# A spectral filter followed by a low-rank token mixer: closing the first group on chip, reading the first weight ahead, and a new schedule for the first two batches

## The chip, the cores and the metric

The kernel runs on one core of one Trainium2 chip. The metric is the device time of one execution in microseconds (us). The trace's span is about 2 us shorter than the time of the same execution. "Step" is the program's own unit: one 512-token first-layer matmul pair with its ReLU, about 1.25 us; eight steps are a token group, six groups (and a shared small one) are a batch.

## The reference, cut to what matters

```python
# batch 8, seq 3136, dim 256; n_freq 1569; rank 32; hidden 1024
X = np.fft.rfft(x, axis=1)
y = np.fft.irfft(X * (filt_r + 1j * filt_i)[None], n=3136, axis=1)
h = y.transpose(0, 2, 1) @ U @ V                 # low rank, along the sequence
u = y + h.transpose(0, 2, 1)
out = u + np.maximum(u @ w_ch1, 0) @ w_ch2
```

The transform of length 3136 is done as 64 x 49 with matrix multiplications in four stages. Stage 1 is the "first weight" product. Then comes a transposition by way of DRAM (`ct1`: store, load back as "turned blocks" `a`); stage 2, the filter product and stage 3; a second pass through DRAM (`ct2`: store from `esb`, load back as `e`); stage 4, the inverse, which gives `ut`, the input of the two-layer network.

## The kernel before

TensorE executes its matmuls in program order. Work of later batches is laid between the network's steps by a plan: `at(step, function)`. The plan fixes only where an instruction stands in each engine's own queue. Batch 0 is different: it is turned on chip, and its filter product is done in an undoubled form.

```python
def load_x(b, c, after=None):          # on GpSimd's queue; converts f32 to f16
    ...
    t = sb.tile([128, 4, XW], F16, tag="x", bufs=4, name="x")
    if after is not None:              # gate: a one-element copy that waits for `after`
        nc.gpsimd.tensor_copy(t[0:1, 0, 0:1], after[0:1, 0:1])
    ...dma_start(...)
...
# batch 0: 16 half blocks; four of the products go to ScalarE + GpSimd
if j in (7, 9, 12, 14):
    nc.scalar.copy(pc, pz); nc.gpsimd.tensor_mul(uv, pc, fin)     # L397
else:
    nc.vector.tensor_mul(uv, pz, fin)                             # L400
...
mid_first()
load_e2(0, 0); load_e2(0, 1)           # from DRAM, after the last store
low_rank(0)
for n, _ in enumerate(st1(1)): ...     # all 13 pieces of batch 1's first weight
keep_warm(6)                           # dummy matmuls, L234
stage4(groups[0], 0); stage4(groups[0], 1)
make_fa(0); make_fa(1)                 # doubled filter matrices fa, fc
...
at(1, make_fa, 2); at(3, make_fa, 3)
at(4, x_after, 2)                      # x of batch 2, gated by groups[0].h[3]
m = later(start[b - 1], (5, -9, -12)[min(b, 3) - 1])   # batch 1's blocks from step 5
z = plan_mid(b, m, (2, 5) if b > 1 else (1, 3, 5))     # those listed: products on GpSimd
```

A block with its products on VectorE takes three 1024-column products (buffers `ta`, `tb`) and one addition on GpSimd. A block on GpSimd is copied out by ScalarE and then needs four GpSimd operations. Both are the doubled form, with matrices `fa` and `fc` that hold the filter twice. The undoubled form of batch 0 takes two products and no addition, but four more 512-column matmuls a block.

Three more words of this text: a bank is one of the eight parts of PSUM, the memory that TensorE writes its results to; an eviction is the copy out of it; the closing is the time from batch 0's last spectral output to the first ReLU.

Of the kernel before, what the change touches and what calls it, by code (L numbers as in the profile page):

```python
# [14 lines left out]
SEQ = 3136  # L15
# [9 lines left out]
def _consts():  # L25
# [10 lines left out]
    wf = np.zeros((128, 25, 128))  # L36
    for h in range(2):
        wf[h::2, 0:24, 64 * h:64 * h + 64] = t1[:, 24 * h:24 * h + 24]
    wf[0:64, 24, 0:64] = t1[:, 48]
# [59 lines left out]
    return (wf.reshape(128, 25 * 128).astype(f16), w2.astype(f16), g3.astype(f16),  # L99
# [4 lines left out]
def kernel(  # L104
# [13 lines left out]
    names = ("wf", "w2", "g3", "s4", "su", "tw", "kr")  # L118
    wf_d, w2_d, g3_d, s4_d, su_d, tw_d, kr_d = (
# [22 lines left out]
    def bank(tag):  # L142
        of = {"m": (0, 1), "o": (2, 3), "w": (4,), "e": (7,), "f": (0, 1, 2, 3, 4, 7), "e0": (7, 4), "f0": (0, 1), "w1": (7, 5, 6)}[tag]
        turn[tag] = turn.get(tag, -1) + 1
        return psum[:, of[turn[tag] % len(of)], :]


    NH = 17
    hring = cst.tile([128, NH, 512], F16, name="hring")
# [3 lines left out]
    wf = cst.tile([128, 25, 128], F16, name="wf")  # L153
    for c in range(4):
        i = slice(8 * c, min(8 * c + 8, 25))
        nc.sync.dma_start(wf[:, i], wf_d.rearrange("p (i m) -> p i m", m=128)[:, i])
# [3 lines left out]
    def load_x(b, c, after=None):  # L160
        if c == 3:
            t = sb.tile([64, DM], F16, tag="xl", bufs=2, name="xl")
            nc.gpsimd.dma_start(t, dram(x.tensor, (b * SEQ + 48) * DM, [[NR * DM, 64], [1, DM]]))
        else:

            t = sb.tile([128, 4, XW], F16, tag="x", bufs=4, name="x")
            if after is not None:
                nc.gpsimd.tensor_copy(t[0:1, 0, 0:1], after[0:1, 0:1])
            for h in range(2):
                nc.gpsimd.dma_start(t[h:128:2, :, 0:2 * DM],  # L170
                                    dram(x.tensor, (b * SEQ + 24 * h + 8 * c) * DM,
                                         [[NR * DM, 64], [2 * DM, 4], [1, 2 * DM]]))
# [6 lines left out]
    def load_filters(a, z):  # L179
# [8 lines left out]
        if z == NK:  # L188
            for p0, src in ((0, filt_r), (64, filt_i)):
# [8 lines left out]
    zero = cst.tile([128, 64], F16, name="zero")  # L198
    nc.vector.memset(zero, 0.0)
    nc.vector.memset(fb[96:128], 0.0)  # L200
    nc.scalar.copy(fb[32:64].rearrange("p s (k f) -> p (s k) f", f=64),
                   free(zero, 32, 64, 0, [[0, NK * DM // 64], [1, 64]]))
    nc.vector.memset(fc[:, 24:29, :], 0.0)
    usb = hflat[0:64, 0:NR * RANK]
    nc.gpsimd.dma_start(usb, moe_U.rearrange("(q r) p -> q (r p)", q=NQ))
# [4 lines left out]

# [7 lines left out]
    nc.scalar.dma_start(g3, g3_d.rearrange("p (f m) -> p f m", f=6))  # L218

# [3 lines left out]
    w2sb = cst.tile([128, 8, DM], F16, name="w2sb")  # L223
    vnat = hflat[64:96, 4704:4704 + SEQ]
    nc.gpsimd.dma_start(vnat, moe_V)
    nc.gpsimd.dma_start(w1sb, moe_w_ch1.rearrange("(h dd) c -> dd h c", h=2))

    sv = cst.tile([96, SEQ], F16, name="sv")
    kr = cst.tile([128, 96], F16, name="kr")

    def keep_warm(n):
        z = bank("f")
        for _ in range(n):
            nc.tensor.matmul(z, wf[:, 0, :], wf[:, 0:4, :].rearrange("p i m -> p (i m)"),  # L234
                             start=True, stop=True)
# [4 lines left out]
    def u_hat():  # L240
        ud = hflat[0:64, 1568:4704].rearrange("q (p c r) -> q p c r", c=2, r=NR)
        for p, eng in ((0, nc.vector.tensor_copy), (16, nc.scalar.copy)):
            eng(ud[:, p:p + 16], bass.AP(tensor=usb.tensor, offset=usb.offset + p,
                                         ap=[list(usb.ap[0]), [1, 16], [0, 2], [RANK, NR]]))
        for p in range(0, RANK, 8):
            z = bank("f")
# [4 lines left out]
            t = [sb.tile([98, NK, 8], F32, tag=tag, bufs=3, name="ut") for tag in ("ta", "tb")]  # L251
# [8 lines left out]
    def st1(b):  # L260
        for c in range(3):
            asb = sb.tile([128, 8, DM], F16, tag="asb", bufs=3, name="asb")
            for j in range(4):
                pf = bank("w" if b > 1 else "w1")
# [5 lines left out]
                if b == 1 and j % 2:  # L270
                    nc.vector.tensor_copy(dst, pf)  # L271
                else:
                    nc.scalar.copy(dst, pf)  # L273
# [5 lines left out]
            if 1 < b < NB - 1 and c:  # L279
                load_x(b + 1, c - 1)  # L280
            yield
        pf = bank("w" if b > 1 else "w1")
        nc.tensor.matmul(pf[0:64, 0:DM], wf[0:64, 24, 0:64], xt[b, 3], start=True, stop=True)
# [3 lines left out]
        if 1 < b < NB - 1:  # L287
# [5 lines left out]
    cm = fc.rearrange("p s d -> p (s d)")  # L293

    def turned(c):
        for g in range(0, 8 if c < 3 else 1, 4):
            for hh in range(2):
                z = bank("f")
                n, o = 512, 3136 * hh + (8 * c + g) * 128
                if c < 3:  # L300
                    for i in range(4):
                        nc.tensor.matmul(z[:, 128 * i:128 * i + 128],
                                         xt[0, c][:, (g + i) // 2, DM * (i % 2) + 128 * hh:DM * (i % 2) + 128 * hh + 128],
                                         wf[:, 8 * c + g + i, :], start=(i == 0), stop=True,
                                         skip_group_check=True)
                else:
                    n = 64
                    nc.tensor.matmul(z[:, 0:n], xt[0, 3][:, 128 * hh:128 * hh + 128],
                                     wf[0:64, 24, 0:64], start=True, stop=True)
                if hh:  # L310
# [3 lines left out]


    esb = {}
# [6 lines left out]
    def out3(b, k, half, pe):  # L323
        if half == 0:
            esb[b, k] = sb.tile([98, 4, DM], F16, tag="esb", bufs=10, name="esb")
        nc.scalar.copy(esb[b, k][:, 2 * half:2 * half + 2, :].rearrange("p s d -> p (s d)"),  # L326
                       pe[0:98])
        if half:
            nc.sync.dma_start(dram(ct2[b], 4 * k * 98 * DM, [[DM, 98], [98 * DM, 4], [1, DM]]),
                              esb[b, k])  # L330

    def stage3(pe, parts, special):

        for n, (v, m, ms) in enumerate(parts):
            kw = dict(start=(n == 0), stop=(n == len(parts) - 1))
            if special:
                nc.tensor.matmul(pe[0:98, 0:DM], g3[:, m, :], v[:, 0:DM], skip_group_check=True, **kw)
        if special:
            for n, (v, m, ms) in enumerate(parts):
                nc.tensor.matmul(pe[0:98, DM:2 * DM], g3[:, ms, :], v[:, DM:2 * DM], start=False,  # L340
                                 stop=(n == len(parts) - 1), skip_group_check=True)
        else:
            for n, (v, m, ms) in enumerate(parts):
                nc.tensor.matmul(pe[0:98], g3[:, m, :], v, start=(n == 0), stop=(n == len(parts) - 1))  # L344
# [8 lines left out]

    def mid_first():
# [3 lines left out]
        def turn_a2(k):  # L358
            z = bank("f0").bitcast(F16)
            for i in range(4):  # L360
                for hh in range(2):
                    nc.tensor.transpose(z[:, DM * i + 128 * hh:DM * i + 128 * hh + 128],
                                        free(fc, 0, 128, 3136 * hh + 4 * k + i, [[32, 128]]), idn)
# [4 lines left out]
            if k in (1, 3):  # L368
                nc.vector.tensor_copy(a2[k], z[0:98])
            else:  # L370
                nc.scalar.copy(a2[k], z[0:98])

        todo = []

        def do3(j, uv):
            pe = bank("e0")
            stage3(pe, [(uv[:, 0], 2, 4), (uv[:, 1], 3, 5)], j == 15)
            out3(0, j // 2, j % 2, pe)

        for k in range(4):  # L380
            turn_a2(k)
        for c in range(4):
            load_x(1, c)
        nc.gpsimd.dma_start(w2sb, moe_w_ch2.rearrange("(cc t) e -> cc (t e)", t=8))
        for j in range(16):
# [6 lines left out]
            fin = free(fb, 0, 128, 2 * j * DM, [[0, 2], [1, 2 * DM]])  # L392
            if j in (7, 9, 12, 14):
                pc = sb.tile([128, 2, 2 * DM], F16, tag="pc", bufs=2, name="pc")
                nc.scalar.copy(pc, pz)
                uv = sb.tile([128, 2, 2 * DM], F16, tag="y", bufs=3, name="uv")
                nc.gpsimd.tensor_mul(uv, pc, fin)  # L397
            else:
                uv = sb.tile([128, 2, 2 * DM], F16, tag="ta", bufs=3, name="uv")
                nc.vector.tensor_mul(uv, pz, fin)  # L400
            if j < 4:
                turn_a2(j + 4)
            todo.append((j, uv))
            if len(todo) > 3:
                do3(*todo.pop(0))
        while todo:
            do3(*todo.pop(0))


    h1 = {}  # L410
# [10 lines left out]
    def low_rank_end(b):  # L421
# [4 lines left out]
        nc.scalar.copy(h1[b][64:96, :], pk[64:96, 0:DM])  # L426
# [5 lines left out]
    def load_e2(b, c):  # L432
# [5 lines left out]
        nc.sync.dma_start(t[0:64], dram(ct2[b], 8 * c * DM, [[NR * DM, 64], [1, n * DM]]))  # L438
# [19 lines left out]
    def stage4(gr, dh):  # L458
# [23 lines left out]
        nc.vector.tensor_copy(o, v)  # L482
# [17 lines left out]
    def mm2_part(gr, t):  # L500
        b = gr.b
        if gr.c == 6:
# [3 lines left out]
            nc.tensor.matmul(o, gr.h[t][:, 0:128], w2sb[:, t, :], start=(t == 0), stop=False,  # L506
# [13 lines left out]
        for tt in range(4 * half, 4 * half + 4):  # L520
            nc.tensor.matmul(o, gr.h[tt][:, i * 128:(i + 1) * 128], w2sb[:, tt, :],  # L521
# [17 lines left out]
    fa = fb  # L539

    def make_fa(i):
        s = slice(8 * i, 8 * i + 8)
        nc.scalar.copy(fc[0:64, s], fb[64:128, s])
        nc.vector.tensor_scalar_mul(fc[64:128, s], fb[64:128, s], -1.0)
        nc.vector.tensor_copy(fa[64:128, s], fb[0:64, s])
        if i == 3:
            nc.vector.tensor_copy(fa[64:65, 31, :], fc[0:1, 31, :])
            for p in (0, 64):
                nc.vector.memset(fc[p:p + 1, 31, :], 0.0)


    keep_warm(10)
    u_hat()
    for c in range(4):
        turned(c)
        keep_warm(2)
    nc.sync.dma_start(sv[0:64], s4_d)
    nc.sync.dma_start(kr, kr_d)
    mid_first()
    load_e2(0, 0)  # L560
    load_e2(0, 1)
    nc.gpsimd.tensor_copy(sv[64:96, :].rearrange("p (r q) -> p r q", q=NQ),
                          vnat.rearrange("p (q r) -> p r q", q=64))
    low_rank(0)
    for n, _ in enumerate(st1(1)):
        if n == 3:
            low_rank_end(0)
        if n == 6:
            put_h(0, 0)
    load_e2(0, 2)  # L570
    load_e2(0, 6)
    keep_warm(6)
    stage4(groups[0], 0)
# [194 lines left out]
```

## Time and profile before

| | before |
|---|---|
| time, median of 3 runs (a fourth came beside the changed kernel) | 557.55 us (556.51 to 558.9) |
| span of the trace | 555.2 us |
| first ReLU | 62.6 us |
| batch 0's groups / batch 1's / the rest | 73.2 / 65.3 / 354.1 us |

The lines are in the prediction. How to read them: a row of forty digits is busy tenths by slice of the span; in a table of stretches each row is one interval with every engine's busy time, the granted TensorE clock and the share of the DMA engines' time; in a timeline the brackets tell how long the engine was idle before the instruction and what ended that.

### The profile page before, as it was taken

To read this page: it belongs to the slowest core of one execution; us is meant where nothing else is said; L and a number is where in the kernel's file an instruction comes from. 1 tells how busy PE (TensorE), PEld (TensorE's weight loads), DVE (VectorE), ACT (ScalarE), POOL (GpSimd) and SP (SyncE) were. 2 spreads that over 40 slices of the span, in tenths; PEclk is the share of its full clock that TensorE was granted. 3 is DMA by queue.
4 is the path that set the end of the run, shared out by engine and by line. 5 is a ranking of instruction groups with operands and counts; after the bars stand their busy time and mean duration, and the time that the engine had idled before them with its cause. 6 is when DMAs were issued, how large, how long until landed. Compare 5 with 4: busy or idle time off the path is not lost.

```text
span 555.2 us, 11638 instructions
## 1 busy us (share of the span) xinstructions
PE 517.2 (93%) x4491; PEld 375.3 (68%) x4491; DVE 353.1 (64%) x409; ACT 390.8 (70%) x684; POOL 282.4 (51%) x194
## 2 busy tenths in 40 slices
PE   5976689997999999999999999999999999999996
PEld 2634356664767777777776777777786777777775
DVE  6764675755756686758846785858746887643332
ACT  8566868774777688767776788677777577765663
POOL 5778179951883165915683175806563297300000
PEclk9999899997999999999999999999999999999999
DMA  9998876894669468774879468865653553333212
GB/s 194 157 170 192 225 141 187 209 230 130 174 184 250 125 176 199 173 204 137 193 222 221 123 173 228 166 199 152 186 170 121 141 167 121 106 113 115 96 77 87
DMA packets 85432, 92.06 MB, mean 166 GB/s; under 512 B 6741, under 2 KB 69416, under 8 KB 85376
## 3 DMA queue, kind: packets, MB, share of 16 engines
q1 hardware_dynamic: 67968, 75.12, 45.5%
q0 software_dynamic: 16960, 15.91, 19.1%
q8 instruction: 35, 0.57, 0.4%
q10 hardware_dynamic: 448, 0.28, 0.3%
q14 instruction: 21, 0.17, 0.1%
HBM read 57.42 MB, written 49.77 MB: 193 GB/s over the span
## 4 chain that ended last, share of the span: by engine, by line
PE 70%; POOL 10%; DVE 7%; DMA 6%; ACT 4%; issue 2%; DVEq 0%; ACTq 0%; POOLq 0%; SPq 0%
PE psum L521 25%; PE psum L488 24%; PE psum L352 4%; PE psum L344 4%; PE psum L477 4%; PE psum L497 3%; PE psum L266 3%; POOL y L634 3%; DMA x<-in_x_dram 3%; POOL x L170 2%; DVE ut L482 1%; DVE tb L632 1%; PE psum L416 1%; DMA w1sb<-in_moe_w_ch_dram 1%; ACT asb L273 1%
## 5 line engine op out<-in xcount | busy, mean ns | idle before, releaser
L492 ACT ACTIVATE hring<-psum 128x512 f16<-128x512 f32 (+1 forms) x416 | 237.7, 576 | 104.5 <-PE psum L488 103.2
L488 PE MATMUL psum<-ut,w1sb 128*128 128x512 f16 (+1 forms) x832 | 240.3, 370 | 6.4 <-ACT hring L492 3.0
L521 PE MATMUL psum<-w2sb,hring 128*128 128x256 f16 x1536 | 230.9, 273 | 0.0
L634 POOL TENSOR_TENSOR y<-ta,tb 128x1024 f16<-128x1024 f16 x56 | 120.5, 2159 | 159.4 <-DVE tb L632 115.5
L521 PEld LDWEIGHTS <-hring 128*128 128x128 f16 x1536 | 143.3, 98 | 63.8 <-issue 3.8
L482 DVE CAST ut<-psum 128x512 f16<-128x512 f32 x96 | 71.1, 741 | 108.3 <-PE psum L477 88.2
L488 PEld LDWEIGHTS <-w1sb 128*128 128x128 f16 x832 | 104.6, 145 | 27.3 <-issue 10.4
L529 DVE COPY och<-psum 128x512 f32<-128x512 f32 x96 | 66.2, 689 | 47.3 <-PE psum L497 46.6
L326 ACT CAST esb<-psum 98x512 f16<-98x512 f32 x128 | 74.7, 586 | 21.6 <-PE psum L344 16.0
L628 DVE TENSOR_TENSOR ta<-psum,fb 128x1024 f16<-128x1024 f32 x41 | 50.0, 1218 | 7.9 <-PE psum L352 6.9
L273 ACT CAST asb<-psum 128x512 f16<-128x512 f32 x78 | 45.7, 589 | 12.3 <-PE psum L266 11.2
L497 PE MATMUL psum<-idn,ut 128*128 128x128 f16 x392 | 54.0, 220 | 0.0
L477 PEld LDWEIGHTS <-e 96*128 96x128 f16 x768 | 35.9, 99 | 25.5 <-issue 10.2
L630 DVE TENSOR_TENSOR tb<-psum,fc 64x1024 f16<-64x1024 f32 x41 | 50.3, 1226 | 0.9
L632 DVE TENSOR_TENSOR tb<-psum,fc 64x1024 f16<-64x1024 f32 x41 | 49.9, 1218 | 0.8
L477 PE MATMUL psum<-sv,e 96*128 96x64 f16 x768 | 38.8, 194 | 6.5 <-DMA e<-ct 3.7
L344 PE MATMUL psum<-y,g 128*98 128x512 f16 x105 | 39.9, 380 | 3.0 <-POOL y L634 1.5
L497 PEld LDWEIGHTS <-ut 128*128 128x128 f16 x392 | 38.4, 98 | 4.9
L628 POOL TENSOR_TENSOR ta<-pc,fb 128x1024 f16<-128x1024 f16 x15 | 32.4, 2159 | 10.7 <-ACT pc L638 10.7
L352 PE MATMUL psum<-a,w2t 98*128 98x512 f16 x113 | 34.3, 379 | 1.7 <-DVE tb L632 1.6
L266 PE MATMUL psum<-x,wf 128*128 128x256 f16 x168 | 31.3, 274 | 2.8 <-DVE asb L271 1.0
L630 POOL TENSOR_TENSOR tb<-pc,fc 64x1024 f16<-64x1024 f16 x15 | 31.8, 2122 | 1.2
(93 smaller groups left out, 373.6 us busy)
## 6 DMA issues: line engine op xcount, KB each, us to landing
out_dram<-och SPq DMA_DIRECT2D x47, 512.0 KB
ct<-esb SPq DMA_DIRECT2D x64, 196.0 KB
x<-in_x_dram POOLq DMA_DIRECT2D x48, 256.0 KB, 8.1
e<-ct SPq DMA_DIRECT2D x48, 256.0 KB
a<-ct SPq DMA_DIRECT2D x56, 196.0 KB
ct<-asb SPq DMA_DIRECT2D x42, 256.0 KB
wf<-wf SPq DMA_DIRECT2D x3, 256.0 KB
w1sb<-in_moe_w_ch_dram POOLq DMA_DIRECT2D x1, 512.0 KB, 6.8
```

The source lines that it names most:

```text
L326: nc.scalar.copy(esb[b, k][:, 2 * half:2 * half + 2, :].rearrange("p s d -> p (s d)"), pe[0:98])
L344: nc.tensor.matmul(pe[0:98], g3[:, m, :], v, start=(n == 0), stop=(n == len(parts) - 1))
L477: nc.tensor.matmul(pu[:, 64 * i:64 * i + 64], e2[b, c][:, i, 128 * dh:128 * dh + 128], sv[:, 64 * r:64 * r + 64], start=(i == 0), stop=Tru ...
L482: nc.vector.tensor_copy(o, v)
L488: nc.tensor.matmul(ph[:, 0:n], w1sb[:, dh, :, t], gr.ut[:, dh, 0:n], start=(dh == 0), stop=(dh == 1))
L492: nc.scalar.activation(h[:, 0:n], ph[:, 0:n], RELU)
L497: nc.tensor.matmul(o[:, dh * 128:dh * 128 + 128], gr.ut[:, dh, t0:t0 + n], idn, start=False, stop=(dh == 1), skip_group_check=True)
L521: nc.tensor.matmul(o, gr.h[tt][:, i * 128:(i + 1) * 128], w2sb[:, tt, :], start=(tt == 0), stop=False, skip_group_check=True)
L529: nc.vector.tensor_copy(gr.och[:, 2 * y:2 * y + 2, :].rearrange("p j d -> p (j d)"), gr.pc)
L628: eng.tensor_mul(ta, p, va)
L630: eng.tensor_mul(tb[0:64], p[64:128], vb[64:128])
L634: nc.gpsimd.tensor_add(ys[k], ta, tb)
```

## The change

The intent: open the first group sooner. (1) The first weight comes compact (410 KB) and is doubled on chip. (2) All 16 products of batch 0 on VectorE. (3) 48 of the 64 blocks of group 0's input come early from DRAM, the last 16 are picked out of SBUF by selection matmuls. (4) Half of batch 1's x and the second layer's weight are loaded behind the low-rank result H; ten pieces of batch 1's first weight move into steps 0 to 10. (5) Batch 1 uses doubled matrices in four blocks only and takes the undoubled form in the other four, at steps 14 to 38. (6) x of batches 2 and 3 is planned at steps 12 to 16 and 40 to 45.

```diff
+    usb = ...; nc.sync.dma_start(usb, ...U...); nc.sync.dma_start(wfc, wf_d)       # compact
+    nc.vector.tensor_scalar_mul(wf[:, :, 64*h:64*h+64], wfc..., <0/1 per partition>)  # doubled
...
+            if j > 13: pick(j - 2)                     # selection matmuls, 4 column strips
+            if k == 5: load_e2(0, 0, 48)               # rows 0 to 47 early
...
+        for dh in range(2): for i in range(8):         # needs the early rows
+            nc.tensor.matmul(pu[dh]..., e2[0, 0][0:48, i, ...], sv[0:48, ...], ...)
+        step1(1); pick(14); low_rank_part(7); pick(15); ...; low_rank_end(0)
+            nc.tensor.matmul(pu[dh], zs[...], s4x, ...)
...
+    load_x(1, 2, h1[0])
+    nc.gpsimd.dma_start(w2sb[:, :, 0:DM], ...)
+    load_x(1, 3)
...
-        lead = (4, 8, 9)[min(b, 3) - 1]
+        if b == 1:
+            for k, q in ((0, 11), (3, 11), (2, 11), (5, 11), (1, 15), (4, 18), (6, 20), (7, 23)):
+                at(q, fetch, k)
+            for k, q, d in ((3, 17, 26), (2, 18, 28), (5, 22, 35), (4, 26, 37)): ...   # doubled form
+            for k, qs in ((0, (14, 15)), (1, (23, 24)), (6, (31, 32)), (7, (35, 36))):
+                ... two_q, mul_q (buffer tag "ta"), three_q                             # undoubled
...
-    at(4, x_after, 2)
+    for n in (0, 0, 1, 1, 2, 5, 6, 7, 8, 10): at(n, step1, 1)
+    for c in range(4):
+        at((12, 13, 15, 16)[c], load_x, 2, c); at((40, 42, 44, 45)[c], load_x, 3, c)
-            plan_st1(b, 12, (0, 1, 3, 4, 5, 7))
+            plan_st1(b, 20, (0, 1, 3, 4, 5, 7))
```

## The prediction

> **What bounds the kernel now.** I read the page first, then the busy time by stretches, then the chain that ended last, then the timeline of the opening. On the page (parts 1 and 2; one digit is 13.9 us):
>
> ```profile
> PE 517.2 (93%) x4491; PEld 375.3 (68%) x4491; DVE 353.1 (64%) x409; ACT 390.8 (70%) x684; POOL 282.4 (51%) x194
> ...
> PE   5976689997999999999999999999999999999996
> ...
> DMA  9998876894669468774879468865653553333212
> ```
>
> TensorE is full from the twelfth slice on. What it isn't, it is in the first six slices (83 us) and in slice ten (125 to 139 us), and there the DMA engines are near full. So there are two places to gain. To see how much, I cut the program at its token groups: eight ReLU steps (the ACT group of L492) make one group; the first group starts at 62.61 us in the timeline, batch 1's first at 135.81, batch 2's at 201.06, and so on. The stretches between those starts, one per batch:
>
> ```profile
> 62.60:135.80 73.20, 60.98 (x499) 42.34 (x498) 49.97 (x61) 51.09 (x88) 47.28 (x33) 0.95 0.76 179
> 135.80:201.05 65.25, 63.77 (x569) 46.98 (x567) 42.89 (x49) 49.37 (x93) 36.11 (x22) 1.00 0.70 182
> 201.05:260.55 59.50, 59.10 (x524) 43.59 (x523) 41.67 (x46) 44.48 (x81) 34.39 (x21) 1.00 0.71 185
> 260.55:323.69 63.14, 62.11 (x558) 46.12 (x557) 43.02 (x49) 47.27 (x91) 34.36 (x21) 1.00 0.72 186
> 323.69:383.20 59.51, 59.08 (x524) 43.56 (x523) 42.24 (x47) 44.48 (x81) 34.41 (x21) 1.00 0.71 183
> ```
>
> Columns: stretch, length, busy of PE, PEld, DVE, ACT, POOL with counts, granted clock, DMA share. Even batches have 48 steps, odd ones up to 56 (8 of them small). A quiet even batch takes 59.5 us with TensorE 99% busy; batch 0 takes 73.2 us although it has fewer TensorE instructions (499 against 524). From 201 us on nothing but TensorE counts.
>
> The time before 62.6 us: the chain that ended last shows what closes batch 0's spectral part and opens the first group:
>
> ```profile
> 47.42 0.61 PE psum L344 x2
> ...
> 48.69 1.08 PE psum L416 x32
> ...
> 57.03 2.72 PE psum L234 x6
> 59.75 0.44 PE psum L477 x8
> 60.21 0.74 DVE ut L482
> ```
>
> Between the last spectral matmul (47.4) and the first use of its result (59.75, L477) lie 12.3 us: the result goes to DRAM and comes back transposed, meanwhile batch 1's first weight product (L266) and six dummy matmuls (L234) fill the time. The product loop before that is uneven:
>
> ```profile
> 29.07 4.70 DVE L400 TENSOR_TENSOR uv<-psum,fb 128x1024 f16<-128x1024 f32 x4 [0.49 <-PE psum L344]
> 34.44 1.23 DVE L400 TENSOR_TENSOR uv<-psum,fb 128x1024 f16<-128x1024 f32 x1 [0.68 <-PE psum L352]
> 36.35 1.22 DVE L400 TENSOR_TENSOR uv<-psum,fb 128x1024 f16<-128x1024 f32 x1 [0.68 <-PE psum L352]
> 39.89 1.22 DVE L400 TENSOR_TENSOR uv<-psum,fb 128x1024 f16<-128x1024 f32 x1 [2.31 <-PE psum L352]
> ```
>
> VectorE does a product in 1.22 us when fed, but from 34 us on it waits, since in-order TensorE waits for the four products on GpSimd, which was itself still issuing DMAs until 36.6. And at the end of batch 0 the chain has the same round trip once more, for batch 1:
>
> ```profile
> 119.15 0.59 ACT esb L326
> ...
> 119.76 6.48 DMA ct<-esb
> ...
> 126.38 3.58 DMA e<-ct
> ...
> 130.09 0.60 PE psum L477 x8
> ```
>
> **What the Trainium skill says.** "TensorE: Matmul & The Clock Gate", Part 1 (the HAM clock gate): after an idle window of about 3.4 us the array runs at half rate. The trace agrees: after these holes the granted clock is 0.50 in 40 to 42 and 58 to 60 us and 0.72 in 130 to 140, and the six dummies took 2.72 us, 0.45 each, where a warm 512-column matmul starts every 0.22. "VectorE: DVE Perf Modes", the perf-mode tier table: a two-input operation with an f32 PSUM operand gets no fast mode, an SBUF f16 copy gets four elements a cycle. It agrees: 1.22 us for 1024 columns against 0.69 for a doubling copy of 2048. "GPSIMD Engine Reference", 4.1: two-input work is about twice as slow there; here 2.12 against 1.22 us. "DMA: Bandwidth & Descriptors", on issuing engines not being separate queues: all DMAs interleave on the same 16 engines; here the store of 119.76, which took 3.3 us from issue to the load behind it at 49.15 to 52.45, took 6.5 when four x loads had been issued at 109 to 112.
>
> **The change part by part.**
>
> 1. Arrival of x of batch 0. The first weight comes as 410 KB and is doubled on chip, instead of 819 KB; the 0.4 MB inverse matrix is asked for only inside the loop; two small constants (some 0.18 MB) are added; U no longer precedes x in the software queue. About 0.45 MB less stands before x; the first 20 us moved about 200 GB/s, so x, last landed at 19.2, lands about 2.2 us earlier. The doubling is two four-mode copies of 1536 columns on VectorE (about 0.55 us each by the 0.69 above), ahead of x. Only two transposed blocks instead of four precede the loop (-1 us), but the last quarter of the low-rank matrix (VectorE, 1.5 us by the row of 2 x 0.54 + 0.42) moves just in front of it. First product: 25.1 to about 22.4, -2.7.
>
> 2. The loop. All 16 products on VectorE: 16 x 1.22 + one block copy 0.69 = 20.2, and 1.8 for the last output matmul and eviction: about 22, against 25.1 to 49.1 = 24.0. TensorE needs per product 0.44 + 0.44, plus 0.67 of transposes in six of them, so it keeps up. -2. Batch 0's output is then whole at about 44.4 (before 49.1). Low-rank matmuls run inside the loop.
>
> 3. The closing. Of the 64 blocks, 48 come from DRAM early: their last store is issued after product 11, about 39; with 3.3 us to land and about 3.5 to load they are in at about 45.5. The last 16 are picked by selection matmuls (64 of 256 columns in four column strips; by L416's 32 in 1.06 us, about 2 us, mostly inside waits), without a round trip. After that: 16 small matmuls 0.8, low-rank eviction 0.37, a matmul 0.3, eviction 0.36, two matmuls with their latency 0.6, ut 0.74, first matmul pair and its latency 0.6, with queueing about 4.5. First ReLU at about 50, before 62.6: from the end of the output 5.6 instead of 13.5 us. Sum of 1 to 3: **-12.6**.
>
> 4. Batch 0's groups. TensorE work: the quiet 59.5, less the second matmuls that group 0 lacks (8 steps x 4 x 0.11 + residuals, -4.0), plus ten pieces of batch 1's first weight moved in here (10 x 0.24 = +2.4), plus the four blocks that use the undoubled filter form, 4 extra 512-column matmuls each (16 x 0.22 = +3.5): 61.4. VectorE: two products instead of three in those blocks saves 4 x 1.22 = 4.9, and the doubling of those four filter blocks goes to GpSimd and past step 30. ScalarE has 48 x 0.6 + 16 x 0.59 + 19 x 0.59 + 2 = 51 us: fits. The last spectral output is at step 38 instead of 40, and x of batch 3 is asked for from step 40 instead of before, so the store should land in about 3.3 instead of 6.5 us; with load about 7 to 8 us in the 8 steps of 1.25 (10 us) that are there. I leave 2.6 us for rough joints, the start with the e loads and w2 above all. 64 instead of 73.2: **-9.2**.
>
> 5. Batch 1: without the half clock in its first 5 us it should come near the other odd batch's 63.1; I take 63.7 for 65.25: **-1.5**. From 201 us the 354.1 us stay: TensorE is full, and 113 instead of 128 partitions change no duration.
>
> Sum: 50 + 64 + 63.7 + 354.1 = 531.8, plus 2.4 between profile span (555.2) and median time (557.55): **534 us**, -4.2%.
>
> **Rivals.** (a) The e load of the first 48 blocks is late. TensorE is in order and the small matmuls that need it stand before the selection matmuls, so each us of delay is one on the path. For: DMA share is about 1.1 in 32 to 46 us, and stores queue behind waits on one queue. Against: half of batch 1's x and w2 are moved out of just this stretch. Worth +3 to +5: 538. (b) The second matmul's weight, issued only when the low-rank result exists, takes 13.6 us to land as it did behind x before, and group 1 waits for it: +2 to +5. Against: then about 1.8 MB of x were queued ahead, now 0.5 MB. (c) The gain of the opening is given back at batch 1's start: the round trip still doesn't fit, or GpSimd, with eight doubling copies and x issues between, is late: +4 to +7, and the clock falls again; about 540. (d) TensorE, now carrying 5.9 us of added matmuls in batch 0, is no worse than before because it was idle there 12 us: that is already in part 4; if the joints are perfect, 530. (e) A quite hidden gain, time unchanged: against it, from 201 us on the chain is TensorE alone, so an earlier start has nowhere to be lost.
>
> **Range and chances.** Parts 1 and 2 I trust to 2 us, 3 to 3, 4 to 4: together some 6. Range 527 to 543. Faster by over 2% needs under 546.4: 0.94; within 2% 0.05; slower 0.01.
>
> **What would show it.** First ReLU at 48 to 53 us; 16 products on VectorE back to back from about 22.4; no dummy matmuls after the loop; granted clock 1.0 after the first 10 us; batch 0's stretch 62 to 67 us; no e wait over 1 us near the start of batch 1; the time from batch 2's start to the end still 354 us. Wrong, if the first ReLU comes after 55, if a wait on DMA of several us stands before L477's successor or the first second matmul, or if the steady batches change.

## The result, and the profile after

The changed kernel took **571.9 us** (570.57 to 573.75, 4 runs); before, beside it, 558.12. Slower by 2.5%: ratio 1.0253, 95% interval 1.021 to 1.0296. Ratios here are the mean time of one kernel's fast runs over that of the other's of the same rounds, so not quite the ratio of the medians.

The page after, parts 1 and 2 (a slice is 14.2 us):

```profile
PE 522.2 (92%) x4535; PEld 374.6 (66%) x4535; DVE 355.9 (63%) x414; ACT 374.9 (66%) x677; POOL 279.2 (49%) x200
...
PE   5897748777899999999999999999999999999997
...
PEclk9896969989999999999999999999999999999999
...
DMA  9996944557769855895489467784755534333212
```

TensorE was busy for only 4 tenths of slice six and 7 to 8 tenths of slices seven to ten; before, these digits were 8, 9, 9, 9 and 7. By stretches, cut at the groups' first ReLUs as before (batch 0, batch 1, batch 2; then groups 1, 3 and 4 of batch 0):

```profile
53.58:149.51 95.93, 69.81 (x534) 46.33 (x533) 52.15 (x65) 48.87 (x87) 43.62 (x37) 0.92 0.70 161
149.51:214.58 65.07, 64.03 (x570) 47.05 (x569) 42.77 (x48) 50.12 (x95) 40.61 (x25) 1.00 0.71 183
214.58:274.14 59.56, 59.17 (x524) 43.54 (x523) 41.62 (x46) 44.53 (x81) 34.41 (x21) 1.00 0.71 184
```

```profile
61.03:83.23 22.20, 11.33 (x81) 7.40 (x81) 9.68 (x18) 5.14 (x9) 1.17 (x2) 0.77 0.79 171
...
95.75:113.08 17.33, 13.23 (x101) 8.74 (x99) 9.10 (x9) 10.52 (x21) 12.65 (x7) 1.00 0.56 153
113.08:132.55 19.47, 15.31 (x104) 9.72 (x102) 9.94 (x12) 11.06 (x21) 4.91 (x6) 0.91 0.50 115
```

The first ReLU does come 9 us sooner (53.59 for 62.61), but batch 0's groups take 95.9 us instead of 73.2; everything later is as long as before (65.1 and 354.5 us). Busy time overstates TensorE's use, since the records of matmuls overlap (L588's last 371 ns each, where a warm one starts every 0.22 us). So I also made an estimate: every matmul at N / 2.4 GHz + 2.5 ns, which the Trainium skill gives for warm matmuls ("TensorE: Matmul & The Clock Gate", Part 1), with 60 columns as the least. A steady batch of 59.5 us comes out at 60.2, so this is good to about 1 us. Batch 0's useful stream rose from 58.3 to 63.6 us; the loss, length less stream, rose from **14.9 to 32.3 us**. By group the loss after is 2.0, 12.9, 1.3, 5.1, 6.9, 4.0 us.

The clock in the closing, by stretches of 2 us (the third figure from the end of a row):

```profile
44.00:46.00 2.00, 0.00 (x0) 0.00 (x0) 0.24 (x1) 0.00 (x0) 0.00 (x0) 0.73 0.75 195
46.00:48.00 2.00, 1.57 (x22) 1.08 (x26) 0.00 (x0) 0.00 (x0) 0.00 (x0) 0.50 0.71 199
...
54.00:56.00 2.00, 2.00 (x10) 1.12 (x9) 1.78 (x3) 0.94 (x3) 2.00 (x3) 0.71 1.15 177
```

Cut finer, it is 1.00 until 44.9, 0.50 until 55.1 and 1.00 again from 55.2 us.

The largest hole, in the timeline of the changed kernel: TensorE, then the sync queue, then GpSimd's queue.

```profile
79.13 1.01 PE L385 MATMUL psum<-a,w2t 98*128 98x512 f16 x2 [10.26 <-DMA a<-ct]
```

```profile
54.80 12.28 SPq L299 DMA_DIRECT2D ct<-asb  x6
67.18 3.02 SPq L537 DMA_DIRECT2D e<-ct  x1
70.31 0.54 SPq L308 DMA_DIRECT2D ct<-al  x1
76.19 1.63 SPq L348 DMA_DIRECT2D a<-ct  x4
```

```profile
57.47 3.74 POOL L187 DMA_DIRECT2D x<-in_x_dram  x6
61.87 0.99 POOL L180 DMA_DIRECT2D xl<-in_x_dram  x1 [0.67 <-DMA w2sb<-in_moe_w_ch_dram]
```

Step 14 needs a turned block of batch 1 and waits 10.26 us for it. The last store of the first weight (32 KB) is issued at 70.31, and the loads behind it may go only at 76.19. Meanwhile the engines carry x of batch 2, the last of which lands at 74.18: GpSimd issues it at 57.5, during step 4, although the plan has it at steps 12 to 16. Nothing tied GpSimd to TensorE's steps there. In the DMA part of the profile between 55 and 79 us the software queue, which carries x and until 61.6 us the second weight, has 61.3% of the engines' time, the hardware queue 36.6%:

```profile
q0 software_dynamic: 2959, 2.28, 61.3%
q1 hardware_dynamic: 3571, 2.32, 36.6%
```

The other holes are of another kind. Timeline of the changed kernel in group 3:

```profile
94.19 4.20 POOL L720 TENSOR_TENSOR y<-ta,tb 113x1024 f16<-113x1024 f16 x2
...
96.34 1.23 DVE L743 TENSOR_TENSOR uv<-psum,fb 113x1024 f16<-113x1024 f32 x1 [1.32 <-ACT hring L592]
97.62 0.59 PE L385 MATMUL psum<-a,w2t 98*128 98x512 f16 x2 [1.53 <-DVE uv L743]
...
98.42 1.22 DVE L743 TENSOR_TENSOR uv<-psum,fb 113x1024 f16<-113x1024 f32 x1 [0.85 <-POOL y L720]
...
104.92 2.12 POOL L720 TENSOR_TENSOR y<-ta,tb 113x1024 f16<-113x1024 f16 x1
107.08 1.22 DVE L714 TENSOR_TENSOR ta<-psum,fb 113x1024 f16<-113x1024 f32 x1 [4.83 <-PE psum L597]
```

Each of these VectorE products starts when a GpSimd addition ends (94.19 + half of 4.20 = 96.29; 98.39; 107.04), whatever the bracket names. All three write a buffer of tag `ta`, and the addition is that buffer's last reader: a block on GpSimd holds a `ta` buffer for some 8 us, and an undoubled block takes two.

At the end of batch 0 TensorE waits for the first turned block of batch 2, while x of batch 3 had been issued from 117.39 on (GpSimd, then TensorE):

```profile
117.39 1.31 POOL L187 DMA_DIRECT2D x<-in_x_dram  x2
```

```profile
139.03 0.59 PE L385 MATMUL psum<-a,w2t 98*128 98x512 f16 x2 [3.04 <-DMA a<-ct]
```

### The profile page after: what moved, and what is told of

Its sections match the earlier page's. It is cut to its first block, busy times and chain, and to the rows that moved or that the text cites. A ratio compares the mean times of both kernels' runs of the same rounds, so it can differ in the third digit from the quotient of the medians.

```text
span 569.1 us, 11725 instructions
## 1 busy us (share of the span) xinstructions
PE 522.2 (92%) x4535; PEld 374.6 (66%) x4535; DVE 355.9 (63%) x414; ACT 374.9 (66%) x677; POOL 279.2 (49%) x200
## 4 chain that ended last, share of the span: by engine, by line
PE 70%; POOL 9%; DMA 7%; DVE 5%; issue 4%; ACT 3%; SPq 0%; ACTq 0%; POOLq 0%; DVEq 0%
PE psum L621 26%; PE psum L588 25%; PE psum L385 4%; PE psum L377 4%; PE psum L597 3%; PE psum L577 3%; PE psum L291 3%; DMA x<-in_x_dram 2%; POOL x L187 2%; POOL y L720 2%; DMA w2sb<-in_moe_w_ch_dram 2%; DMA a<-ct 1%; POOL sv L464 1%; PE psum L515 1%; DVE tb L718 1%
## 5 line engine op out<-in xcount | busy, mean ns | idle before, releaser
L588 PE MATMUL psum<-ut,w1sb 128*128 128x512 f16 (+1 forms) x832 | 241.4, 371 | 1.9 <-DVE ut L582 1.1
L720 POOL TENSOR_TENSOR y<-ta,tb 113x1024 f16<-113x1024 f16 x52 | 112.1, 2161 | 146.0 <-DVE tb L718 129.9
L582 DVE CAST ut<-psum 128x512 f16<-128x512 f32 x94 | 69.7, 741 | 98.6 <-PE psum L577 82.4
L588 PEld LDWEIGHTS <-w1sb 128*128 128x128 f16 x832 | 104.6, 145 | 24.4 <-issue 6.8
L295 ACT CAST asb<-psum 128x512 f16<-128x512 f32 x76 | 44.9, 590 | 22.1 <-PE psum L291 21.1
L385 PE MATMUL psum<-a,w2t 98*128 98x512 f16 x120 | 37.9, 394 | 21.6 <-DMA a<-ct 13.3
L714 DVE TENSOR_TENSOR ta<-psum,fb 113x1024 f16<-113x1024 f32 x37 | 45.1, 1219 | 16.6 <-PE psum L385 7.7
L714 POOL TENSOR_TENSOR ta<-pc,fb 113x1024 f16<-113x1024 f16 x15 | 32.3, 2155 | 34.2 <-ACT pc L724 34.2
L716 DVE TENSOR_TENSOR tb<-psum,fc 49x1024 f16<-49x1024 f32 x37 | 45.4, 1226 | 0.9
L718 DVE TENSOR_TENSOR tb<-psum,fc 49x1024 f16<-49x1024 f32 x37 | 45.1, 1218 | 1.0
L377 PE MATMUL psum<-y,g 113*98 113x512 f16 x98 | 37.4, 382 | 2.1 <-ACT esb L355 1.1
L577 PE MATMUL psum<-sv,e 96*128 96x64 f16 x752 | 37.3, 192 | 1.6 <-ACT asb L295 1.6
L291 PE MATMUL psum<-x,wf 128*128 128x256 f16 x168 | 33.1, 281 | 2.3 <-DVE ut L582 1.9
L716 POOL TENSOR_TENSOR tb<-pc,fc 49x1024 f16<-49x1024 f16 x15 | 31.8, 2120 | 1.2
```

Of the source, the lines that this page charges most:

```text
L385: nc.tensor.matmul(pz, w, a, start=True, stop=True)
L577: nc.tensor.matmul(pu[:, 64 * i:64 * i + 64], e2[b, c][:, i, 128 * dh:128 * dh + 128], sv[:, 64 * r:64 * r + 64], start=(i == 0), stop=Tru ...
L582: (nc.scalar.copy if gr is groups[0] and dh else nc.vector.tensor_copy)(o, v)
L588: nc.tensor.matmul(ph[:, 0:n], w1sb[:, dh, :, t], gr.ut[:, dh, 0:n], start=(dh == 0), stop=(dh == 1))
L714: eng.tensor_mul(ta, p[0:NZ], va)
L716: eng.tensor_mul(tb[0:NR], p[64:NZ], vb[64:NZ])
```

## The experiments

"Before" was run beside each of them (medians 555.95 to 557.08 us). Losses and stretches are from each run's own trace, one per edit. The changed kernel was not run beside them, so compare the ratios; the intervals of e1 (1.0106 to 1.0237) and e11 (1.0113 to 1.0281) overlap its own, and what these two show is in their traces.

| run | edit | median us | ratio to before | first ReLU | batch 0's groups |
|---|---|---|---|---|---|
| changed kernel | | 571.9 | 1.0253 | 53.6 | 95.9 |
| e1 | x of batch 2 gated | 566.8 | 1.0172 | 52.9 | 92.2 |
| e2 | own buffer for GpSimd blocks | 563.6 | 1.0114 | 52.3 | 89.7 |
| e3 | e1 + e2 | 561.2 | 1.0067 | 53.6 | 86.7 |
| e4 | e load behind the last store | 571.1 | 1.0249 | 53.0 | 96.9 |
| e5 | e3, six evictions to VectorE | 562.3 | 1.0118 | 53.7 | 86.3 |
| e6 | e3, batch 1's x early | 559.0 | 1.0059 | 58.0 | 79.4 |
| e7 | e5 + e6 | 557.4 | 1.0029 | 56.4 | 79.6 |
| e8 | new opening, schedule of before | 570.0 | 1.0251 | 60.0 | 87.1 |
| e9 | e2, and loads put around the round trips | 552.2 | 0.9926 | 54.0 | 76.4 |
| e10 | e9, other steps for the single bank | **550.1** | **0.9899** | 53.8 | 74.6 |
| e11 | changed kernel, no selection matmuls | 567.6 | 1.0197 | 53.2 | 90.2 |
| e12 | e10, no selection matmuls | 555.7 | 1.0001 | 52.8 | 76.8 |

**e1, e2, e3, e4: the two holes and a rival for the first.** Theory A: x of batch 2, issued ten steps early, fills the DMA engines while batch 1's first product makes its round trip. Rival B: the last store merely stands behind an e load in the sync queue. Theory C: shared product buffers. Rival D: VectorE is overfull.

```diff
# e1
-        at((12, 13, 15, 16)[c], load_x, 2, c)
+        at(15, x_after, 2, c)        # load_x(2, c, groups[1].h[7] if c == 0 else None)
-            plan_st1(b, 20, (0, 1, 3, 4, 5, 7))
+            plan_st1(b, 21, (0, 1, 3, 4, 5, 7))
# e2
-            box[k] = [pz] + [sb.tile(..., tag="ta", bufs=3, name="ta"), tbs[...]]
+            pool = k in ((3, 5) if b == 1 else on_pool)
+            ta = sb.tile(..., tag="tp" if pool else "ta", bufs=1 if pool else 3, name="ta")
# e4
-        at(8 * c - 14, load_e2, 0, c)
+        at(12 if c == 3 else 8 * c - 14, load_e2, 0, c)
```

> Edit: the x loads of batch 2 on GpSimd's queue get a gate (they wait for the ReLU of step 15, i.e. until the first use of batch 1's turned blocks), batch 2's first weight starts at step 21 instead of 20. Theory A (GpSimd, which nothing holds back, issues these 1.5 MB at 57.5 us, ten steps ahead of the plan, and they fill the DMA engines while batch 1's first product makes its round trip): TensorE's wait of 10.3 us for the turned block falls to 2 to 4 us, the clock stays at 1.0 there, time about 571.9 - 9 = 563 us (560 to 566). Rival B (the store of the last block stands behind the e load on the sync queue, whatever else runs): the wait stays at 8 us or more, time within 3 us of 572. Theory C (shared product buffers) touches only what comes after 90 us: the waits there stay.

> Edit: only the blocks whose products run on GpSimd get a buffer of their own for the first product; the VectorE products keep the three of before. Theory C (the slow GpSimd blocks hold the three buffers which the undoubled blocks on VectorE now take twice each): VectorE's waits of 1.3, 0.85 and 4.8 us at 96, 98 and 107 us go, TensorE's behind them (1.5 at 97 and part of 110 to 116) too: -3 to -6 us, about 567; the wait of 10.3 us at 69 us is as before. Rival D (those holes come from VectorE being overfull, with negations slowed by GpSimd): within 2 us of 572.

> Edits of e1 and e2 together. If A and C are both right and independent: about 572 - 9 - 4.5 = 558.5 (554 to 562), still not faster than before by 2%, since a wait of about 3 us for the turned block and the crowded end of batch 0 stay. If A alone holds: as e1.

> Edit: one e load (group 3 of batch 0) is planned at step 12 instead of 10, so that it no longer stands before the store of batch 1's last first-weight block on the sync queue; x of batch 2 ungated. Rival B: the store is issued about 3 to 5 us earlier and TensorE's wait of 10.3 falls by that, about 567 us. Theory A: the two large stores of 64.2 and 64.9 us are stuck in the full DMA engines anyway, the wait stays at 8 us or more, time 570 to 573.

In e1 (566.58 and 567.08 us) TensorE's line at step 14 reads

```profile
73.39 1.01 PE L385 MATMUL psum<-a,w2t 98*128 98x512 f16 x2 [5.58 <-DMA a<-ct]
```

so the wait fell from 10.26 to 5.58 us and the time by about 5, less than the 9 I expected. In e4 it stayed at 9.00 (571.15 and 571.14 us), though the store was issued 3.9 us sooner, at 66.43: the loads behind it still went only at 75.93. In e1, without x, they went 4.1 us after it (66.27 to 70.39). So what holds them is the traffic in front, not the place of the small store. Theory A is right in direction and rival B falls, but A is only half of the hole: with x out of the way, one round trip still doesn't fit into the four steps from 10 to 14. In e2 (563.27 and 563.96 us) groups 3 and 4 fell from 36.8 to 30.9 us, the wait at step 14 stayed (10.20). That is theory C, somewhat stronger than expected. The edit adds a fourth buffer, so it shows that buffers were short; whether three unshared ones would do is not tested. 1.3 us of e2's gain is an earlier first ReLU, which the edit doesn't explain: in its trace the clock fell at 47.9 us instead of 44.9, so that more of the closing ran at full clock. Both together (e3) gave 561.2, not the 558.5 of the sum. (A version of e2 with three more buffers did not fit into SBUF.)

**e5, e6, e7: what is left in e3?** Theory E: ScalarE is crowded. Theory G: half of x behind H leaves the round trip too few steps.

```diff
# e5, on e3: batch 2's first weight, six of twelve evictions to VectorE
+ {1: (0, 3, 4, 5, 7, 8, 9, 11), 2: (3, 4, 6, 9, 10, 11)}
# e6, on e3
-        for c in range(2): load_x(1, c)
+        for c in range(4): load_x(1, c)
-    load_x(1, 2, h1[0]) ... load_x(1, 3)
-    for n in (0, 0, 1, 1, 2, 5, 6, 7, 8, 10): at(n, step1, 1)
+    for n in (0, 0, 1, 1, 2, 2, 3, 3, 4, 5): at(n, step1, 1)
```

> Edit on top of e3 (561.2 us): six of the twelve evictions of batch 2's first weight go from ScalarE to VectorE. Theory E (the packed schedule gives ScalarE three evictions in many of the steps 20 to 38, 1.8 us of work against 1.25 us of TensorE's, and in-order TensorE waits for their banks): groups 3 to 5, 14.6 + 16.6 + 17.8 = 49.0 us in e3, fall by 3 to 5, time about 557. Rival F (the pair of product banks and VectorE set the pace there, not ScalarE): groups 3 to 5 within 1.5 us of 49 or longer, time 560 to 563.

> Edit on top of e3: the second half of batch 1's x is loaded ahead of the low-rank result again, and the ten remaining pieces of batch 1's first weight stand at steps 0 to 5 instead of 0 to 10. Theory G (half of x behind H leaves the round trip of batch 1's first product only four steps): TensorE's wait of 5.2 us for the turned block goes (under 1 us), group 1 falls from 16.3 to about 11; the e load of the closing meets the x load and the first ReLU comes 1 to 3 us later than 53.6. Time about 557 (555 to 559). Rival: the gain is all given back in the closing (first ReLU at 58 or later), time 560 to 563.

> Edits of e5 and e6 together on top of e3: about 561 - 4 - 4 = 553 us if both theories are right, 557 if one, 561 if none.

e5: groups 3 to 5 took 14.80 + 17.40 + 17.55 = 49.75 us against 49.04 in e3, the time 561.53 and 563.07. Theory E falls. e6: the wait at step 14 is gone and group 1 took 9.3 instead of 16.3 us, so G is right about that; but the closing paid:

```profile
50.85 1.03 PE L486 MATMUL psum<-sv,e 48*128 48x64 f16 x16 [9.03 <-DMA e<-ct]
```

This is the wait for the early rows of group 0, 2.99 us in the changed kernel, 9.03 here. The sync queue of e6 shows why: a store issued at 37.77 lets the load behind it go only at 47.74, while batch 1's x and the second weight are in flight.

```profile
37.77 1.22 SPq L362 DMA_DIRECT2D ct<-esb  x1
47.74 0.32 SPq L537 DMA_DIRECT2D e<-ct  x1
```

In the changed kernel the same pair is 39.40 and 43.48 us. So "half of x behind H" does what it was meant to do for the closing. Its price is the late first weight. e7 (557.53 and 557.21 us) confirms both: no wait at step 14, first ReLU at 56.4.

**e8: the new opening with the old schedule.** All of x early, all blocks doubled in otherwise idle time, blocks at steps 6 to 41 much as before.

```diff
+        for k in range(8): make_fc(k, nc.gpsimd.tensor_copy)     # inside the product loop
+        for _ in range(5): step1(1)                              # in the closing
+        for k in range(8): make_neg(k)
+    for k in range(8): make_fa(k, nc.vector.tensor_copy)
-        if b == 1: ...                                           # the undoubled schedule
+    at(6, x2_all)                                                # gate groups[0].h[5]
```

> The new opening and closing of batch 0 with the schedule of before behind it: all of batch 1's x early, its first weight done in the hole of the closing and steps 0 to 1, all filter blocks doubled (on GpSimd inside the product loop, on VectorE in the closing) and none taken in the undoubled form, batch 1's spectral blocks at steps 6 to 41, x of batch 2 gated at step 6, x of batch 3 where the change has it, own buffer for the GpSimd blocks. Theory H (the opening is worth its 9 us, and what was lost is the schedule of batch 0 behind it): first ReLU 54 to 57 us, the stretch of batch 0 68 us or less (before 73.2, changed kernel 95.9), time 540 to 549, faster than before by 1.5 to 3%. Rival I (an earlier first group only moves the wait: batch 0's groups stay as long as before because the DRAM round trips of batch 1 and not TensorE set them): stretch of batch 0 as long as the ReLU came earlier, time 555 to 560.

It took 569.96 us (567.41 to 571.6), a miss. Groups 1 to 4 were short, 44.7 us (46.1 before), and the useful stream of batch 0 was back at 58.9 us from 63.6: by the same estimate 3.5 us of this are the 16 matmuls of the undoubled form, and 1.1 us are five pieces of first weight that e8 has in the closing. But all three round trips met a load, and TensorE waited

```profile
52.31 1.03 PE L492 MATMUL psum<-sv,e 48*128 48x64 f16 x16 [7.94 <-DMA ct<-esb]
...
76.91 1.01 PE L385 MATMUL psum<-a,w2t 98*128 98x512 f16 x2 [8.82 <-DMA a<-ct]
...
135.06 1.01 PE L385 MATMUL psum<-a,w2t 98*128 98x512 f16 x2 [7.24 <-DMA a<-ct]
```

24 us in all. Rival I, that an earlier start only moves the wait, described this better than theory H, though the time lies outside both ranges.

**e9 and e10: each load placed where no round trip is open.** x stays behind H, but its last rows come ahead of the second weight; the first weight ends at step 6, blocks are fetched at 9, x of batch 2 is gated at 10, batch 2's first fetches come a step earlier. e10 also moves batch 2's first weight off the step ahead of stage 4, which uses the same single bank.

```diff
-    nc.gpsimd.dma_start(w2sb[:, :, 0:DM], ...)
     load_x(1, 3)
+    nc.gpsimd.dma_start(w2sb[:, :, 0:DM], ...)
-    for n in (0, 0, 1, 1, 2, 5, 6, 7, 8, 10): at(n, step1, 1)
+    for n in (0, 0, 1, 1, 2, 4, 4, 5, 5, 6): at(n, step1, 1)
+        at(10, x_after, 2, c)        # gate groups[1].h[2]
-((0, 11), (3, 11), (2, 11), (5, 11), ...
+((0, 9), (3, 9), (2, 9), (5, 9), ...
-            at(later(s, -3 if b == 2 else -9), fetch, k)
+            at(later(s, -4 if b == 2 else -9), fetch, k)
-            plan_st1(b, 20, (0, 1, 3, 4, 5, 7))
+            plan_st1(b, 17, (0, 1, 3, 4, 5, 7))      # e10: (0, 2, 3, 4, 6, 7)
```

> Candidate, x still behind H: the own buffer of e2; the last rows of batch 1's x loaded ahead of w2 instead of behind it, so that its first weight ends at step 6 instead of 10; turned blocks fetched at step 9; x of batch 2 gated at step 10, its first weight from step 17; batch 2's first fetches one step earlier. Theory A/G (each DRAM round trip that other loads run into costs its delay, and only that): first ReLU 53 to 54.5, no wait over 1 us for the turned block at step 14, that of batch 2 (2.7 us in e3) under 1; stretch of batch 0 about 77 (e3 86.7), time 550 to 553, faster than before by under 2%. Rival: w2, now behind, holds group 1 for 2 us or more, or x of batch 2 meets the fetch again (wait over 3 us): 555 to 560.

> As e9, but batch 2's first weight in the steps 0, 2, 3, 4, 6, 7 of a group instead of 0, 1, 3, 4, 5, 7: not in the step just ahead of the inverse transform, which uses the same single bank. The trace of e3 shows 2.2 us of TensorE waits there between 91 and 122 us (inverse transform behind that eviction). Theory F (single banks in an in-order engine set the rest of the loss): 1.5 to 2.5 us less than e9, about 549. Rival: those waits move to the next user of the bank, within 1 us of e9.

e9 took 552.2 us (551.05 to 554.71): no wait for the block at step 14, none for batch 2's block. e10 took **550.13** (549.98 to 552.82), ratio 0.9899, interval 0.9842 to 0.9956: faster than both kernels, by 1% over before, which is clear of noise but under 2%. Its stretches for batches 0 to 2:

```profile
53.77:128.32 74.55, 65.89 (x532) 44.98 (x531) 51.85 (x65) 48.55 (x87) 43.34 (x39) 0.99 0.87 202
128.32:193.64 65.32, 64.32 (x573) 47.34 (x571) 42.81 (x48) 50.23 (x96) 40.89 (x25) 1.00 0.74 188
193.64:253.18 59.54, 59.15 (x524) 43.54 (x523) 41.59 (x46) 44.52 (x81) 34.43 (x21) 1.00 0.71 184
```

Batch 0 is 21 us shorter than in the changed kernel; its loss is 11.1 us (3.1, 0.6, 1.7, 1.5, 3.4, 0.8 by group). The 2 us between e9 and e10 are about as large as the runs' spread, so the single bank as their cause is likely, not shown.

**e11 and e12: without the selection matmuls.** The first group then waits for all 64 blocks by way of DRAM. The edit also takes the early e loads out of the sync queue and the low-rank matmuls out from behind their wait.

```diff
-            if j > 13: pick(j - 2)
-                if k == 5: load_e2(0, 0, 48)        # and the loads of k == 6
+                if k == 7: load_e2(0, 0); load_e2(0, 1)
-        pick(14) ... pick(15), zs, s4x matmuls; the e matmuls moved behind low_rank_end, rows 0:64
```

> The changed kernel without its selection matmuls: the first group waits for all 64 blocks by way of DRAM, behind the last store, the rest unchanged. The prediction's part 3 would have this closing 4 to 6 us longer (first ReLU at 58 to 60 instead of 53.6). Rival J (the early 48 blocks, stored at 39.4 and in only at 46.4, set the closing anyway; the last store is asked for only 5 us later): first ReLU 1 to 3 us later, at 55 to 56.5. The time is blurred by the waits behind; 572 to 576.

> e10 without the selection matmuls (e11's edit). If they only replace one wait by an equal one (e11: first ReLU 53.2 against 53.6), first ReLU at 53 to 54 us and the time within 2 us of e10's 550.1; the x loads behind H then start some 7 us earlier and meet the closing's e loads, so that the first ReLU may come up to 1 us later and w2 earlier. If the selection matmuls do save a round trip when nothing else is in the way, 553 or more.

e11's first ReLU came at 53.18 us: not later at all, even beyond rival J. (Batch 0's output was whole at 41.55 us, in the changed kernel's trace at 43.40: there the clock was at half from 21.1 to 24.4 us, as in some runs and not in others. In e1, e3, e9 and e10, which have the selection matmuls and the output whole at 41.5 to 41.8, the first ReLU came at 52.9 to 54.0, so e11 is no later than these either.) Its wait

```profile
49.69 1.03 PE L487 MATMUL psum<-sv,e 64*128 64x64 f16 x16 [6.72 <-DMA e<-ct]
```

ends 3.3 us later than that for the early rows (46.42), but the low-rank work is done by then instead of queued behind. In the changed kernel the early load stands in the sync queue waiting for its store (39.40 to 43.48 us) and holds back the last two stores to 43.90 and 44.78; e11 issues these at 39.81 and 41.58 and asks for the whole block at 44.44. e11 is also 4 us faster in median, with 4.7 us between its two runs (565.25 and 569.96 us), so the time alone doesn't show it; in the trace H is done earlier, opens the gate of batch 1's x at 43.8 instead of 50.8, x of batch 2 is through by 65.7 instead of 74.2, and the wait at step 14 is 5.32. On the better schedule the same edit (e12) came out 1% behind e10 (0.9953 to 1.0049 for 0.9842 to 0.9956, the intervals just touch): 551.56 to 558.01 us, median 555.69, a wide spread. By what I wrote beforehand (553 or more) that speaks for the selection matmuls. But in the profiled run, the fastest, the first ReLU is as early (52.75), and TensorE loses its time later, with a 1.67 us wait for the turned block at step 14 that e10 doesn't have. The slower runs have no trace. What the selection matmuls are worth on this schedule, and with x held back otherwise, stays open.

## Why the prediction was wrong

- **Parts 1 and 2, opening and loop: right.** First product at 21.48 us (predicted 22.4), loop over at 42.1, output whole at about 43.4 (predicted 44.4), with all products on VectorE in 1.22 us and nearly back to back. (The granted clock, forecast at 1.0 after the first 10 us, was 0.50 from 21.1 to 24.4 us.)

- **Part 3, the closing: mechanism wrong, size off by 3.6 us.** The early rows were in at 46.4, 0.9 us later than estimated. But in the wait for them, 2.99 us, the clock fell: it is 0.50 from 46 to 54 us, so the whole closing chain, sized warm, ran at half clock and took 7.2 instead of 4.5 us. No run has this chain at full clock throughout; in e2, where the clock fell 2.9 us later, it took 6.1. So the clock is the likely cause; that it makes all of the 2.7 us is not shown. I named the clock gate for other holes and did not apply it to this one, which my own working contained. I also read those holes wrongly when I wrote that the trace agrees with an idle window of 3.4 us: before the fall at 57.1 us in the kernel before, the longest hole is 1.02 us, and before the fall at 39.9 us it is 2.46. And e11 shows that the selection matmuls were not needed for the gain: without them the first ReLU comes as early.

- **Part 4, batch 0's groups: the step that failed.** I wrote 61.4 us of TensorE work and "2.6 us for rough joints". The growth is borne out: the stream grew by 5.3 us (predicted +5.9 for moved pieces and undoubled blocks), though it came to 63.6 us, 2.2 more than written. The second, the joints, measured 32.3 us of loss: this is the term that failed. Three parts of it were missing:
  - *Batch 1's round trip, 12.9 us in group 1.* I took the plan's step for the time of a DMA. An ungated load on GpSimd starts when GpSimd is free, here at 57.5 us; the gate of before was dropped by the change, and I did not notice. I also overlooked that the first undoubled block stands at step 14, four steps behind the last piece of first weight. e1 shows the first cause (wait 10.3 to 5.6), e6 and e9 the second (wait gone). What of the 12.9 us is not the wait itself came with it: the clock was at half from 72.2 to 82.5 us.
  - *Shared buffers, about 6 of the 12 us lost in groups 3 and 4.* I credited the undoubled form with 4.9 us of VectorE time and did not ask where its results are kept. e2 shows it. The other 6 us of these groups are not explained; e5 only rules out that six evictions on ScalarE made them.
  - *The end of batch 0, 4.0 us.* The prediction said x of batch 3 would now stay clear. It was planned at step 40 and issued at 117.4, about step 33. The wait was for batch 2's turned block (3.04 us), issued at 135.32 behind batch 1's e load (134.08); whether x of batch 3 made that late was not tested apart. With the fetch a step earlier in the sync queue (e9, with the rest of its edits) the loss there fell to 0.8.

- **Part 5 and the rest: right for the rest (354.5 for 354.1), 1.4 us off for batch 1** (65.1 for 63.7): the half clock was not what made it longer than another odd batch.

- **The rivals.** (a), a late e load, came to 0.9 us, not 3 to 5. (c), "given back at batch 1's start", had the right mechanism, a round trip that doesn't fit, but at the wrong round trip and at 4 to 7 us. (b), w2 late, cost 0.63 us. (e), no place where the gain could be lost, was wrong in its argument: batch 0's own groups are such a place.

The miss adds up: first ReLU 3.6, batch 0 31.9, batch 1 1.4, the rest 0.4, difference of span and median 0.4: 37.7 us, and 534.2 + 37.7 = 571.9.

## What to carry to other kernels

A position in the program is not a time: for every DMA ask what makes its queue wait, and give a large load a gate so that it can't start while a small store and load on the critical path are open. When work moves later, count the steps that its round trip has left, and how many buffers each form of the work holds and for how long. A short hole is paid twice when it lets the TensorE clock fall, so size the chain behind it at half pace.

## What the Trainium skill lacked or had wrong

- "DMA: Bandwidth & Descriptors", Queues, rings and completion order (Arbitration): each engine goes round-robin between queues. It gives no size for what a small transfer pays beside a full software queue. Here the loads went 5.8 us after the 32 KB store before them with x in flight, and 4.1 after it without (e1); after a 196 KB store it was 10.0 us (e6, 37.77 to 47.74) instead of 4.1. The software queue had 61.3% of the engines' time from 55 to 79 us.
- "TensorE: Matmul & The Clock Gate", Part 1, says that the clock falls after at least one idle window of about 3.4 us. Here it fell sooner: at 44.9 us, 1.5 us after the last matmul; at 116.6 after a hole of 2.52 us; and at 57.1 in the kernel before, where no hole in the 3.4 us ahead is over 1.02 us and TensorE was busy for half of them. (The same page names frequent short gaps as a second cause, without a size.)
- The same page says that it comes back after at least one busy window of about 3.4 us, and not when it takes more. After the falls at 21.1 and 116.6 us it was back 3.4 us later. After the fall at 44.9 it took 10.2 us, with TensorE busy 1.6 to 2.0 of every 2 us from 46 us on; in e2 the fall in the closing lasted 6.9 us.
- No page says that in a plan of interleaved work GpSimd's DMAs run ahead of TensorE's steps unless something holds them: loads planned at steps 12 to 16 were issued in step 4.
